# Memory attention and an erf-softplus FFN on one core: batch 0's keys before its values, tokens in chunks of 116 and 112, all heads' sums in one group

## The chip, the cores and the metric

The kernel runs on one core of one Trainium2 chip. TensorE (PE) multiplies, VectorE (DVE), ScalarE (ACT) and GpSimd (POOL) work elementwise, and SyncE (SP) issues the loads and stores, which 16 DMA engines carry out. The metric is the time of one execution on the device in microseconds, lower is better.

## The reference

Eight batches of eight heads, 576 tokens and head size 64 go through an attention over 32 memory slots, and the result through a feed-forward layer with 2048 hidden values.

```python
a = exp(phi - max(phi, axis=2)); a = a / (sum(a, axis=2) + 1e-09)     # phi: b h s 32, max and sum over tokens
k_m = einsum('bhsm,bhsd->bhmd', a, k)
v_m = einsum('bhsm,bhsd->bhmd', a, v)
scores = scale * (q @ k_m.T)                                           # b h s 32
attn = softmax(scores, axis=-1)
x = (attn @ v_m), heads side by side                                   # 4608 x 512
h = x @ w_in                                                           # 4608 x 2048
g = h * erf(softplus(h))
out = g @ w_out                                                        # 4608 x 512
```

Everything is 32-bit floats, and so are the matmuls in effect: most of them are made of three products of high and low parts (`_hi`, `_lo`), some of full 32-bit operands ("exact").

## The kernel before, in words

The kernel is written as a list of operations, each with an engine, a cost in ns, a rank, and the tiles that it reads and writes. A planner (`Plan.order`) plays them through with these costs, always takes the ready operation of lowest rank on the engine that is free first, keeps count of the buffers of each kind (`room`), and so fixes the order of the instructions on every engine before the kernel is built. On the chip each engine runs its list strictly in that order and waits where an operand isn't there. While the first output matmul has not been placed, TensorE's expected gaps are filled with matmuls on zeros (`fill`, L365).

`FIRST` (L821) is the order of the first loads: phi transposed (two halves of the heads), phi, the keys and values of head pairs 0 and 1 (`kv0`, `kv1`), the first eighth of w_in, `kv2`, `kv3`, the queries of the batch's two token halves, then the second eighth of w_in and the first of w_out. All loads and stores are issued by SyncE. A `kv` tile holds keys and values of two heads, `[128, 5, 2, 2, 64]`; `load_tokens` (L393) puts tokens 0 to 511 four to a partition (one piece of 4 KB each) and the last 64 tokens into a fifth chunk of 64 partitions.

`memories` (L485) computes a batch's k_m and v_m: the maxima of phi (L491), exponentials (L514, L516, L521), and then `one_memory` (L530) once for each group of four heads: the sums over tokens on TensorE (L540, five chunks by four heads, keys and values side by side in 128 columns, each head to its own 32 rows of the result), a scaled eviction by ScalarE (L550) and a copy (L552), two transposes (L557), and four evictions into `km` and `vm` (L570, L573). The 32-bit product of one matmul is two instructions, so that a group's sums are 40. For batches 1 to 7 this is done while the FFN of earlier batches runs, and the rank puts it well ahead of its use.

`attention` (L616) makes the scores of one token half (L583 of `q` and `km`) and its softmax, nearly all on VectorE (L629 to L650). `vw` (L594) multiplies `w_in` by `v_m` (L583 of `w_in` and `vm`), so that the FFN's first product is `attn @ (v_m @ w_in)`, `ffn1` (L681). The weights come as 64-bit floats and are turned into 32-bit ones (`decode`: L429, L443, L465 on VectorE, L435, L439 on ScalarE). Softplus and erf are ScalarE's (L704, L709); `g_split` multiplies and splits; `ffn2` (L754) sums the output of 512 tokens of each batch over 16 steps, and `ffn2_rest` the remaining 64 tokens of two batches together from `rest`. For the first 16 steps (`FR2`) these 64 columns are gathered by POOL in `rest_f` (L723) and split by `rest_split` (L745 on ScalarE, L748 on VectorE). `store` evicts and issues the output: into one of two `ot` tiles by ScalarE, and in the last batch in two halves, by ScalarE (L800) and VectorE (L803).

Buffers that matter here: `raw` (four) holds phi, `kv`, later queries, and one part of w_out (`wf`) until `split_wo` has split it; `wo` (eight) holds the weights, and at the start also `kv3` and the first queries; `phiT` has two, `ot` two, and `ps`, the result banks of all small products, four.

Of the kernel before, what the change touches and what calls it, by code (L numbers as in the profile page):

```python
# [237 lines left out]
def tile_memory_attention_then_erf_softplus_ffn(  # L238
# [10 lines left out]
    nc = tc.nc  # L249
# [16 lines left out]
    SC = [(c * P, min(P, S - c * P)) for c in range((S + P - 1) // P)]  # L266
    RAW = 4
# [10 lines left out]
        for n, b, kw in (  # L278
# [9 lines left out]
            ("ot", 2, {}),  # L288
# [6 lines left out]
    room.update({"g_hi": 3, "g_lo": 3, "raw": RAW, "ot": 2, "ps": 4, "sc": 2, "dk": 1, "phiT": 2})  # L295
    room.update({f"pso{d}": 1 for d in range(NT)})
    for n in ("pmx", "psm", "prs"):
# [10 lines left out]
        "ot": ("ot", [P, DM], F32),  # L308
# [18 lines left out]
    def mm(n, exact):  # L327
        return 2 * (2 * n / 2.4 + 2.5) if exact else n / 2.4 + 11.7
# [10 lines left out]
    zeros = const.tile([P, 512], BF16, name="zeros")  # L339
# [21 lines left out]
    def fill(n):  # L361
        if n and not idle:
            idle.append(pools["po"].tile([P, DM], F32, name="idle", tag="pso0"))
        for _ in range(n):
            nc.tensor.matmul(out=idle[0], lhsT=zeros[:, :P], rhs=zeros, start=True, stop=True)  # L365


    def load(rank, key, nbytes, emit):
        op(SP, 60, rank, [], [key], emit, nbytes=nbytes)

    def load_weight(rank, name, c):
# [14 lines left out]
        load(rank, key, P * 8192, emit)  # L386

    def load_phiT(rank, b, g):
        key = tile_("phiT", "phiT", b, g)
        load(rank, key, P * S * 4,  # L390
             lambda: nc.sync.dma_start(out=get(key), in_=phiT[b, g * P : (g + 1) * P, :]))

    def load_tokens(rank, key, src, n_bytes, view):  # L393
        n = S // P
        load(rank, (key, "whole"), S // P * P * n_bytes, lambda: nc.sync.dma_start(
            out=view()[:, :n], in_=src[: n * P].rearrange("(p c) e -> p c e", c=n)))
        load(rank + 0.001, (key, "last"), SC[-1][1] * n_bytes, lambda: nc.sync.dma_start(
            out=view()[: SC[-1][1], n], in_=src[n * P :]))

    def load_phi(rank, b):  # L400
        key = tile_("raw", "phi", b, shape=[P, len(SC), H * M], pool="raw")
        load_tokens(rank, key, phi[b], H * M * 4, lambda: get(key))

    def load_kv(rank, b, p, tag="raw"):
        key = tile_(tag, "kv", b, p, shape=[P, len(SC), 2, 2, D], pool=tag)
        load_tokens(rank, key, kv[b, p], 4 * D * 4,
                    lambda: get(key).rearrange("p c x h d -> p c (x h d)"))

    def load_q(rank, u, tag="raw"):
        key = tile_(tag, "q", u, shape=[P, NP_, U], pool=tag)  # L410
        b, hf = divmod(u, 2)
        load(rank, key, P * NP_ * U * 4, lambda: nc.sync.dma_start(
# [72 lines left out]
    def memories(rank, rank_2, b):  # L485
        a = ("phi", b)
        n, ln = S // P, SC[-1][1]
# [11 lines left out]
        def turn():  # L499
            for g in range(NG):  # L500
# [5 lines left out]
        op(DVE, on_dve(n * H * M), rank, [(a, "whole"), ps], [(a, "whole")],  # L506
           lambda: nc.vector.tensor_tensor(
               out=get(a)[:, :n], in0=get(a)[:, :n],
               in1=get(ps).unsqueeze(1).to_broadcast([P, n, H * M]), op=ALU.add))
        op(DVE, on_dve(H * M), rank, [(a, "last"), ps], [(a, "last")],  # L510
           lambda: nc.vector.tensor_tensor(
               out=get(a)[:ln, n], in0=get(a)[:ln, n], in1=get(ps)[:ln], op=ALU.add))
        op(ACT, on_act(n * H * M), rank, [(a, "whole")], [(a, "whole")],
           lambda: nc.scalar.activation(get(a)[:, :n], get(a)[:, :n], AF.Exp), kind="exp")  # L514
        op(ACT, on_act(H * M), rank, [(a, "last")], [(a, "last")],
           lambda: nc.scalar.activation(get(a)[:ln, n], get(a)[:ln, n], AF.Exp), kind="exp")  # L516
# [10 lines left out]
        for g in range(NG):  # L527
            one_memory(rank_2 + g * 0.01, b, g)

    def one_memory(rank, b, g):  # L530
        a, rs = ("phi", b), ("prs", b, g)
# [180 lines left out]
    def g_split(rank, i):  # L712
# [3 lines left out]
        if i < FR2:  # L716
            t = tile_(("g_hi", "g_lo")[i % 2], "g", i, shape=[P, S], pool="g")
            r = ("rest_f", k // 8)
            if k % 8 == 0:
                tile_("ot", *r)  # L720
# [88 lines left out]
    def at(step):  # L809
        return 100 * step  # L810
# [136 lines left out]
```

## Time and profile before

| | us |
|---|---|
| median of 3 runs | 731.06 (730.51 to 731.53) |
| profiled execution, its own time | 729.75 |
| its span, first to last instruction | 728.0 |

The span is cut by the profile into what each engine did and into the chain of work that ended last, followed back from the last instruction. The granted clock of TensorE is 0.999 of full speed in this execution. Times in the rows are microseconds from the span's start, means of groups are in ns; L540 is line 540 of the kernel. A matmul's row has the shape of the array that it uses (128\*128, 128\*32, 64\*32) and the elements that it produces; `x40` counts instructions. The matmuls on zeros at the start count as busy time.

### The profile page before, as it was taken

What the parts mean: (1) busy time and instruction counts of PE and PEld (TensorE: products, weight loads), DVE (VectorE), ACT (ScalarE), POOL (GpSimd) and SP (SyncE); (2) the same over time, 40 slices, a digit from 0 to 9 for tenths busy, and PEclk for the clock granted to TensorE, in tenths of its full rate; (3) what the DMA queues carried; (4) which work ended last, traced back from release to release, by engine and by line L of the source; (5) the groups of instructions that cost most, each with busy time, mean ns of one, the idle gap of its engine ahead of it and who ended that gap; (6) DMA issues with size and microseconds to landing.
All of it is one profiled execution on the core that took longest, in us unless ns stands there. A gap on an engine that the chain in (4) does not pass through costs nothing.

```text
span 728.0 us, 12307 instructions
## 1 busy us (share of the span) xinstructions
PE 720.0 (99%) x4816; PEld 553.8 (76%) x4816; DVE 521.0 (72%) x963; ACT 449.9 (62%) x708; POOL 98.7 (14%) x246
## 2 busy tenths in 40 slices
PE   9999999999999999999999999999999999999997
PEld 4456555578887888888788887888878788888885
DVE  3899999689677685877755587777854587666631
ACT  5799999875747666594644556474754266454611
POOL 0011001120111111111111011111111111111110
PEclk9999999999999999999999999999999999999999
DMA  9996332421503115111310214211210100010002
GB/s 321 391 389 227 100 149 82 161 100 43 173 24 108 42 39 178 35 59 34 107 57 1 91 48 127 70 59 33 66 33 1 59 15 0 1 45 15 1 1 72
DMA packets 30393, 64.75 MB, mean 89 GB/s; under 512 B 2688, under 2 KB 13440, under 8 KB 29312
## 3 DMA queue, kind: packets, MB, share of 16 engines
q1 hardware_dynamic: 30336, 63.97, 26.1%
q8 instruction: 38, 0.62, 0.4%
q14 instruction: 19, 0.16, 0.1%
HBM read 54.53 MB, written 9.44 MB: 88 GB/s over the span
## 4 chain that ended last, share of the span: by engine, by line
PE 87%; DMA 6%; ACT 4%; DVE 1%; SPq 1%; issue 1%
PE pso L754 48%; PE psh L681 26%; PE psr L754 6%; PE psa L583 5%; DMA w<-w_in 4%; PE psa L540 2%; DMA kv<-kv 2%; ACT w L439 1%; ACT w L435 1%; ACT e L709 0%; ACT L709 0%; PE psa L557 0%; ACT e L704 0%; DVE w L443 0%; ACT vw_hi L354 0%
## 5 line engine op out<-in xcount | busy, mean ns | idle before, releaser
L754 PE MATMUL pso<-wo,g_hi 128*128 128x512 f32 x896 | 280.8, 395 | 0.0
L704 ACT ACTIVATE e<-h 128x576 f32<-128x576 f32 x128 | 88.0, 687 | 171.5 <-DVE h L696 170.9
L754 PEld LDWEIGHTS pso<-wo,g_hi 128*128 128x128 f32 x896 | 160.0, 188 | 31.8 <-issue 6.3
L754 PE MATMUL pso<-wo,g_lo 128*128 128x512 f32 x448 | 176.1, 393 | 0.0
L696 DVE COPY h<-psh 128x288 f32<-128x288 f32 x239 | 107.8, 452 | 42.8 <-PE psh L681 41.2
L681 PE MATMUL psh<-at_hi,vw_hi 128*128 128x288 f32 x496 | 113.7, 310 | 0.0
L681 PE MATMUL psh<-at_hi,vw_lo 128*128 128x288 f32 x496 | 106.0, 295 | 0.3 <-DVE vw_lo L356 0.3
L681 PE MATMUL psh<-at_lo,vw_hi 128*128 128x288 f32 x496 | 106.1, 295 | 0.0
L681 PEld LDWEIGHTS psh<-at_hi,vw_hi 128*128 128x128 f32 x496 | 84.5, 188 | 27.8 <-issue 8.2
L735 POOL CAST rest<-g_hi 128x64 fp32r<-128x64 f32 x112 | 51.1, 457 | 391.3 <-DVE g_hi L730 385.5
L728 DVE TENSOR_TENSOR e<-e,h 128x576 f32<-128x576 f32 x112 | 82.7, 751 | 26.5 <-ACT e L709 26.4
L754 PEld LDWEIGHTS pso<-wo,g_lo 128*128 128x128 f32 x448 | 84.1, 188 | 19.2
L730 DVE CAST g_hi<-e 128x576 fp32r<-128x576 f32 x112 | 50.7, 457 | 63.1 <-PE pso L754 51.1
L731 DVE TENSOR_TENSOR g_lo<-e,g_hi 128x576 fp32r<-128x576 f32 x112 | 86.3, 771 | 4.4
L709 ACT ACTIVATE e<-e 128x576 f32<-128x576 f32 x128 | 80.3, 675 | 0.4
L681 PEld LDWEIGHTS psh<-at_hi,vw_lo 128*128 128x128 f32 x496 | 79.8, 188 | 0.7 <-DVE vw_lo L356 0.5
L681 PEld LDWEIGHTS psh<-at_lo,vw_hi 128*128 128x128 f32 x496 | 79.1, 188 | 0.0
L735 POOL CAST rest<-g_lo 128x64 fp32r<-128x64 f32 x112 | 37.8, 338 | 110.8 <-DVE g_lo L731 103.7
L754 PE MATMUL pso<-w,g 128*128 128x512 f32 x112 | 52.5, 599 | 0.0
L754 PE MATMUL psr<-wo,rest 128*128 128x512 f32 x192 | 49.0, 390 | 0.0
L354 ACT ACTIVATE vw_hi<-psa 128x512 fp32r<-128x512 f32 (+1 forms) x68 | 34.9, 556 | 19.6 <-PE psa L583 19.5
L356 DVE TENSOR_TENSOR vw_lo<-psa,vw_hi 128x512 fp32r<-128x512 f32 (+1 forms) x68 | 42.0, 632 | 6.5 <-ACT vw_hi L354 6.3
(82 smaller groups left out, 716.0 us busy)
## 6 DMA issues: line engine op xcount, KB each, us to landing
kv<-kv SPq DMA_DIRECT2D x32, 512.0 KB, 4.2
q<-qT SPq DMA_DIRECT2D x16, 576.0 KB, 5.0
w<-w_in SPq DMA_DIRECT2D x8, 1024.0 KB, 11.6
w<-w_out SPq DMA_DIRECT2D x8, 1024.0 KB, 11.2
out<-ot SPq DMA_DIRECT2D x32, 256.0 KB, 2.0
phiT<-phiT SPq DMA_DIRECT2D x16, 288.0 KB, 2.9
phi<-phi SPq DMA_DIRECT2D x8, 512.0 KB, 5.7
kv<-kv SPq DMA_DIRECT2D x32, 64.0 KB, 4.2
```

The lines of the kernel that those rows point to most:

```text
L354: lambda: nc.scalar.activation(get_hi(), get_src(), AF.Identity))
L356: lambda: nc.vector.tensor_tensor(out=get_lo(), in0=get_src(), in1=get_hi().bitcast(F32), op=ALU.subtract))
L583: nc.tensor.matmul(out=get(ps[par])[p * M : (p + 1) * M, :], lhsT=w()[rows, p, :], rhs=x()[rows, p, :], start=True, stop=True,)
L681: nc.tensor.matmul(out=get(ps), lhsT=x[:, g, k % 4 * P : (k % 4 + 1) * P], rhs=y[:, g, :], start=(n + g == 0), stop=(n == len(parts) - 1 a ...
L696: lambda: nc.vector.tensor_copy(out=keep(), in_=get(ps)),
L704: last[:] = [op(ACT, on_act(S), rank, [("h", i)], [e], lambda: nc.scalar.activation(get(e), get(("h", i)), AF.Softplus), kind="softplus", ...
L709: last[:] = [op(ACT, on_act(S), rank, [e], [e], lambda: nc.scalar.activation(get(e), get(e), AF.Erf), kind="erf", edge=edge, after=last)]
L728: op(DVE, on_dve(S), rank, [e, h], [e], lambda: nc.vector.tensor_tensor(out=get(e), in0=get(e), in1=get(h), op=ALU.mult))
L730: op(DVE, on_dve(S, 1), rank, [e], [hi], lambda: nc.vector.tensor_copy(out=get(hi), in_=get(e)))
L731: op(DVE, on_dve(S), rank, [e, hi], [lo], lambda: nc.vector.tensor_tensor(out=get(lo), in0=get(e), in1=get(hi).bitcast(F32), op=ALU.subtract))
L735: lambda x=x, y=y: nc.gpsimd.tensor_copy(out=rest[:, k, x, cols], in_=get(y)[:, NT * P :]))
L754: nc.tensor.matmul(out=o, lhsT=y, rhs=z, start=(start and n == 0), stop=(stop and n == len(parts) - 1))
```

## The change

Tokens are laid out in five chunks of 116, 116, 116, 116 and 112 rows: 112 partitions get five tokens each, and the last 16 tokens go to four more partitions with four each. In batch 0 keys and values of a head pair are loaded separately (pieces of 512 bytes), in the order keys, queries, values, with the first eighth of w_in ahead of the keys; `one_memory` takes a list of parts (head group, keys or values), and in batch 0 sums all heads' keys first and all heads' values second, in later batches both groups, keys and values, at once. The evictions of a part write each 64 columns twice side by side, which takes the place of the copy L552, and the evictions into `km` and `vm` take both groups. `raw` has five buffers. The `ot` tiles are gone: outputs pass through `phiT` tiles, and the last batch's stores are one ScalarE copy. `rest_split` is gone: POOL writes the high part of the 64 columns and subtracts for the low part. The planner's cost of a 512-column matmul is 15.5 ns above its columns instead of 11.7.

```diff
-    SC = [(c * P, min(P, S - c * P)) for c in range((S + P - 1) // P)]
-    RAW = 4
+    NC = (S + P - 1) // P
+    FULL = S // NC // 16 * 16
+    MORE = FULL + (S - FULL * NC) // (NC - 1)
+    RAW = 5
...
-    room.update({"g_hi": 3, "g_lo": 3, "raw": RAW, "ot": 2, "ps": 4, "sc": 2, "dk": 1, "phiT": 2})
+    room.update({"g_hi": 3, "g_lo": 3, "raw": RAW, "ps": 4, "sc": 2, "dk": 1, "phiT": 2})
...
-        return 2 * (2 * n / 2.4 + 2.5) if exact else n / 2.4 + 11.7
+        return 2 * (2 * n / 2.4 + 2.5) if exact else n / 2.4 + (15.5 if n == DM else 11.7)
...
+    def load_tokens(rank, key, n_bytes, src, dst, what=None):
+        n = FULL * NC
+        load(rank, n * n_bytes, [(key, (what, "whole")), (key, (what, "last"))],
+             lambda: nc.sync.dma_start(out=dst(slice(0, FULL), slice(0, NC)), in_=src(slice(0, n), NC)))
+        load(rank + 0.001, (S - n) * n_bytes, [(key, (what, "more"))],
+             lambda: nc.sync.dma_start(
+                 out=dst(slice(FULL, MORE), slice(0, NC - 1)), in_=src(slice(n, S), NC - 1)))
...
-        for g in range(NG):
-            one_memory(rank_2 + g * 0.01, b, g)
+        for turn_n, part in enumerate(parts):
+            one_memory(rank_2 + turn_n * 0.01, b, part)
...
+            for n, g in enumerate(gs):
+                for c in range(NC):
+                    ln = MORE if c < NC - 1 else FULL
+                    for j in range(4):
+                        h = 4 * g + j
+                        nc.tensor.matmul(
+                            out=get(ps)[M * j : M * (j + 1), n, : n_x * D],
+                            lhsT=get(a)[:ln, c, h * M : (h + 1) * M],
+                            rhs=get(("kv", b, h // 2))[:ln, c, x0, h % 2 * D : (h % 2 + 1) * D],
+                            start=(c == 0), stop=(c == NC - 1))
...
+            part = [(("rest", k, x), b % 2) for x in range(2)]
+            op(POOL, 400, rank, [t], part[:1], lambda: nc.gpsimd.tensor_copy(
+                out=rest[:, k, 0, cols], in_=get(t)[:, NT * P :]))
+            op(POOL, 400, rank, [t, part[0]], part[1:], lambda: nc.gpsimd.tensor_tensor(
+                out=rest[:, k, 1, cols], in0=get(t)[:, NT * P :],
+                in1=rest[:, k, 0, cols].bitcast(F32), op=ALU.subtract))
...
-    def rest_split(rank, q):
...
-        t = tile_("h" if final else "ot", "ot", *o)
-        halves = [(0, DM // 2, ACT), (DM // 2, DM, DVE)] if final else [(0, DM, ACT)]
+        t = tile_("h" if final else "phiT", "ot", *o)
+        op(ACT, on_act(DM, True), rank - 30, [o], [t],
+           lambda: nc.scalar.activation(get(t)[:, :DM], get(o), AF.Identity))
...
-    FIRST = ["phiT0", "phiT1", "phi", "kv0", "kv1", "in0", "kv2", "kv3", "q0", "q1", "in1", "out0"]
+    BOTH = [(0, 0), (0, 1)], [(1, 0), (1, 1)]
+    TOGETHER = [tuple(BOTH[0] + BOTH[1])]
+    EARLY = [((0, 0), (1, 0)), ((0, 1), (1, 1))]
+    FIRST = ["phiT0", "phiT1", "phi", "in0", "k0", "k1", "k2", "k3", "q0", "q1", "v0", "v1", "v2", "v3"]
+    FIRST += ["in1", "out0"]
...
-    memories(at(-10), at(-9), 0)
+    memories(at(-10), at(-9), 0, EARLY)
...
-        when(n, memories, at(n), at(n + 3), b)
+        when(n, memories, at(n), at(n + 3), b, TOGETHER)
```

176 lines of the change are left out of this document (81 added, 95 removed).

## The prediction

> **What bounds the kernel now.** I read the page first: the span, the busy line and the chain that ended last.
>
> ```profile
> span 728.0 us, 12307 instructions
> ...
> PE 720.0 (99%) x4816; PEld 553.8 (76%) x4816; DVE 521.0 (72%) x963; ACT 449.9 (62%) x708; POOL 98.7 (14%) x246
> ...
> PE 87%; DMA 6%; ACT 4%; DVE 1%; SPq 1%; issue 1%
> ```
>
> TensorE bounds it: 99% busy, and 87% of the chain that ended last is its own work. But the busy share also counts the matmuls on zeros that fill the start (L365), so the start has to be read by itself, from the timeline of TensorE and of VectorE up to 60 us.
>
> ```profile
> 20.19 0.84 PE L583 MATMUL psa<-q,km 64*32 64x288 f32 x16 [0.29 <-DMA q<-qT]
> 22.09 7.73 PE L365 MATMUL idle<-zeros 128*128 128x512 bf16 x35
> 29.66 4.04 PE L681 MATMUL psh<-at,vw_hi 128*128 128x288 f32 x16
> 48.76 1.88 PE L754 MATMUL pso<-w,g 128*128 128x512 f32 x4
> ...
> 21.87 1.37 DVE L632 TENSOR_REDUCE smx<-sc 128x18 f32<-128x576 f32 x2
> 28.26 1.43 DVE L650 STREAM_TRANSPOSE at<-sc 128x576 f32<-128x576 f32 x2
> 31.31 1.22 DVE L465 SCALAR_TENSOR_TENSOR w_in<-w 128x1024 int32<-128x1024 int32 x1
> ```
>
> The columns are start, length, engine, line, operation, tiles, count, and in brackets the idle time and what ended it. The second half of the queries ends the wait at 20.19; then VectorE works through the softmax until 29.69, and only then does the first FFN matmul run. The output matmuls begin at 48.76. So there are two stages: a start of 48.8 us set by loads and by VectorE, and some 679 us in which TensorE is the limit and every microsecond taken off it is a microsecond of time. In that second stage I read the chain in order of time (start, length, what), around the sums of batch 3.
>
> ```profile
> 180.05 1.02 PE psa L583 x16
> 181.07 1.36 PE psa L540 x40
> 182.43 0.90 PE pso L754 x3
> 183.33 0.80 PE psh L681 x6
> 184.13 0.69 PE pso L754 x3
> ...
> 189.27 0.22 PE psa L557 x2
> 189.49 0.69 PE pso L754 x3
> 190.18 1.36 PE psa L540 x40
> 191.54 1.59 PE pso L754 x6
> 193.13 0.22 PE psa L557 x2
> ```
>
> All of it is TensorE, without a gap: two bursts of sums (L540, 40 instructions each) and two pairs of transposes (L557). Three output matmuls take 0.69 us elsewhere and 0.90 us right after a burst (six: 1.59 against 1.38), so leaving a burst costs 0.21 us more. The weight loads show what is inside one burst.
>
> ```profile
> 181.00 0.81 PEld L540 LDWEIGHTS psa<-kv,phi 128*32 128x32 f32 x32 [0.84 <-ACT e L709]
> 182.01 0.15 PEld L540 LDWEIGHTS psa<-kv,phi 64*32 64x32 f32 x8 [0.20 <-issue]
> 182.36 0.30 PEld L754 LDWEIGHTS pso<-wo,g_hi 128*128 128x128 f32 x2 [0.20 <-issue]
> ```
>
> The 32 of the four full chunks go at 0.81 / 32 = 25.3 ns each. Then 0.20 us pass before the 8 of the 64-row chunk (array shape 64*32 instead of 128*32), which go at 18.8 ns, and another 0.20 us before the array is back at 128*128. The 64-row chunk costs 0.35 us of a burst's 1.36, for a tenth of the tokens.
>
> The timeline of TensorE has one pair of transposes like this.
>
> ```profile
> 189.10 0.38 PE L557 MATMUL psa<-ident,kvk 128*128 128x128 f32 x2
> 189.24 0.70 PE L754 MATMUL pso<-wo,g_hi 128*128 128x512 f32 x2
> ```
>
> **The change part by part.** *Sums of batches 1 to 7 in one burst, no 64-row chunk.* Before, per batch: 2 x (1.36 + 0.21) for sums and 2 x 0.22 for transposes = 3.58 us. After: 80 instructions of 116 or 112 rows, all in the shape 128*32. I price them like the 32 full ones, 80 x 25.3 ns = 2.02 us, plus one 0.20 us on leaving, plus 0.21 us of slower output matmuls once. The four transposes stand together: a pair costs 0.22, of which about 0.08 is paid on entering and leaving (the timeline rows above: a pair gives way after 0.14 us, the rest of the 0.22 falls on the matmul after it), so four cost 0.36. Sum 2.79; saved 0.79 per batch, 5.5 us over seven. The bound from below is that only one leave and one pair's entry go and the 80 instructions still take 2 x 1.36: 0.29 per batch, 2.0 us. From above: 0.1 us more per batch for one entry fewer, 6.2 us. I take 5.5, because the 25.3 ns stands in the same burst.
>
> [...]
>
> *What the one burst waits for.* It needs `phi` and all four `kv` tiles at once, all five `raw` slots where it was three tiles for the first burst. A late tile stops TensorE in its order, as one did:
>
> ```profile
> 129.16 1.42 PE L540 MATMUL psa<-kv,phi 128*32 128x128 f32 x36 [0.58 <-DMA kv<-kv]
> ...
> 141.83 0.69 PE L583 MATMUL psa<-q,km 64*32 64x288 f32 x16
> ...
> 149.14 0.62 PE L754 MATMUL pso<-wo,g_hi 128*128 128x512 f32 x2
> ```
>
> Nothing for it in the sum: the sums of batch 3 run at 181 to 192, and TensorE has FFN work that can stand ahead. If that cover is gone it is 0.58 us and more each. In batch 2 the tile `wf` holds a slot too; its sums can only come later than now (121 to 130), after `split_wo` of the last part has freed it. They precede that batch's first queries (141.83 now, which then move as well), and its FFN follows 16 steps behind batch 1's, whose output matmuls begin at 149.14; a step is 2 x 0.80 + 4 x 0.69 = 4.4 us, so there is room. That the wait at 129.16 disappears would give up to 0.6; I count 0.
>
> *The start.* Ahead of the softmax stood phiT 0.59, phi 0.59, keys and values 2.36, the first w_in 1.05 and the queries 1.18 MB. The values' 1.18 MB now come behind the queries. What that is worth, and what the smaller pieces cost, I take from the packets of three windows of the DMA view (15.6 to 17.2, 15 to 16 and 23.4 to 25 us):
>
> ```profile
> DMA packets 498, 0.57 MB, mean 357 GB/s; under 512 B 15, under 2 KB 497, under 8 KB 497
> ...
> DMA packets 286, 0.33 MB, mean 333 GB/s; under 512 B 2, under 2 KB 284, under 8 KB 286
> ...
> q1 hardware_dynamic: 286, 0.33, 106.5%
> ...
> DMA packets 292, 0.63 MB, mean 393 GB/s; under 512 B 3, under 2 KB 3, under 8 KB 286
> ...
> q1 hardware_dynamic: 292, 0.63, 104.3%
> ```
>
> 1.18 MB at 357 GB/s are 3.3 us. The pieces become 512 B (one of keys or values of two heads per token), 2304 of them for the keys, 144 on each of 16 engines. A packet took 1.065 x 16 x 1000 / 286 = 59.6 ns at 1.15 KB and 1.043 x 16 x 1600 / 292 = 91.4 ns at 2.16 KB; the line through both gives 39 ns at 512 B, so 5.6 us for the keys, 2.3 more than at 357 GB/s. The other end is no loss at all. The share above 100% says that the packets overlap and their times are overstated, so I take the middle, 1.1 us for keys and 1.1 for values. The softmax then starts 3.3 - 1.1 = 2.2 us earlier, and all loads behind the values come 2.2 us later. [...]
>
> SyncE issues 16 loads for batch 0's keys and values instead of 8; the second of w_in is queued behind them, and the transfers ahead of it cover the issuing. That w_in is decoded by VectorE at 31.31, after the softmax, so 2.2 us of delay on its landing are hidden. Values at 20.3 + 2.2 us still leave 5 us for their sums, turns and the first `vw`, needed at 29.66 - 2.2. Then VectorE is busy without a break, which lets the gain of 2.2 pass on to 48.76; but ScalarE waits for the fourth w_in:
>
> ```profile
> 28.01 10.14 DMA w<-w_in
> ...
> 38.17 1.11 ACT w L435
> ```
>
> That load comes 2.2 us later, and 1.5 us earlier because batch 1's first `kv` (0.59 MB) no longer finds a free `raw` slot ahead of it: +0.7. Between -2.2 and +0.7 I take -1.2 us for the start, nearer to VectorE's end, since it is VectorE that has no gap there.
>
> *The end.* The last store was VectorE's half, then ScalarE's:
>
> ```profile
> 723.37 0.43 DVE ot L803
> ...
> 723.83 0.38 ACT ot L800
> ...
> L800 ACT ACTIVATE ot<-psr 128x512 f32<-128x512 f32 x3 | 1.7, 581 | 0.0
> ```
>
> 0.84 us becomes one ScalarE copy of 0.58: -0.25.
>
> *Hidden.* `rest_split` goes (two of 0.62 us on ScalarE, two of 0.68 on VectorE), and 16 POOL subtractions come, each behind its copy; bounded by that copy's 0.6 us and its double, on an engine 14% busy, for a result that is read a batch later. ScalarE's 12 evictions of a batch become 6 wider ones on an engine 62% busy. Stores take their tile from the `phiT` slots: a phiT load now waits behind four stores, on SyncE's queue, with `kv` and queries behind it; it is needed a batch later, so 0, and if that cover goes it is the 0.58 us kind of wait above. A planner price of 15.5 instead of 11.7 ns moves orders only.
>
> Sum: -5.5 - 1.2 - 0.25 = -6.95 us. On the profiled execution's 729.75 us (span 728.0) that is 722.8; the median of three runs stands 1.31 higher, so **724.1 us**.
>
> **The rivals.** *Steady gain only.* The fourth w_in sets the start: +0.7 instead of -1.2, 726.0 us. For it: the chain runs through that load. Against: VectorE has no gap from 21.87 on. *The burst does not shrink*, the change not doing what it says: the pace of 80 is set by something other than the shape. 2.0 + 1.2 + 0.25: 727.6 us. Against: the 0.20 us gaps stand on both sides of the 64*32 rows. *The loads go one by one.* By landing times,
>
> ```profile
> kv<-kv SPq DMA_DIRECT2D x32, 512.0 KB, 4.2
> ...
> phiT<-phiT SPq DMA_DIRECT2D x16, 288.0 KB, 2.9
> ```
>
> eight loads of 287 KB at 2.9 us instead of four at 4.2: 6.4 us more until the weights, less 1.5, +4.9 at the start: 731.06 - 5.75 + 4.9 = 730.2 us. Against: 357 GB/s flowed with loads of this size queued behind each other. [...] *Slower: the burst waits for its fourth `kv` tile in every batch.* The tile takes 4.2 us from issue to landing and its slot comes free late, so TensorE stands in its order; from 1.0 us a batch (6.95 / 7) this eats all, and at 1.5 us it gives 724.1 + 10.5 = 734.6 us. For it: 129.16. Against: one such wait in the whole trace. *More:* the start follows by 3.3 and the wait at 129.16 goes: 721.4 us.
>
> **How the numbers follow.** Forecast 0.48, steady only 0.20, burst as before 0.10, more 0.07, one by one 0.06, slower 0.09. Range 720.5 to 729.5 holds all but the last two. Within 0.2% (1.46 us, about what can be told from no change) lies one by one alone: faster 0.85, same 0.06, slower 0.09.
>
> **What would show it.** L540 without any 64*32 form, 80 in one piece of about 2.2 us, and 0.90 us after it only once a batch; the wait for queries ending near 18 us and the first L681 near 27.5; L754 from about 47.5; no L803 at the end. Wrong would be: `kv` as releaser of L540 in several batches, L754 starting after 49, or bursts of 2.7 us.

## The result, and the profile after

The changed kernel is slower: 735.91 us (median of 10 runs, 733.23 to 739.67) against 731.6 us of the kernel before in the same session, a ratio of 1.0065 with a 95% interval of 1.0043 to 1.0086. The forecast was 724.1 us. The profiled execution took 736.58 us by itself. The page of the changed kernel, its span, busy line and shares of the chain that ended last:

```profile
span 734.6 us, 12406 instructions
...
PE 715.7 (97%) x4877; PEld 555.8 (76%) x4877; DVE 518.4 (71%) x955; ACT 435.4 (59%) x654; POOL 101.1 (14%) x262
...
PE 91%; DMA 7%; SPq 0%; ACT 0%; DVE 0%; issue 0%; ACTq 0%
```

TensorE is still the limit of nearly all of it. The timeline of TensorE shows where it is behind (in the new kernel the sums are L563, the transposes L586, the small products L616, the first FFN product L714, the output matmuls L773):

```profile
13.77 0.30 PE L563 MATMUL psa<-kv,phi 116*32 116x64 f32 x4 [0.78 <-ACT w L452]
14.87 0.75 PE L563 MATMUL psa<-kv,phi 116*32 116x64 f32 x36 [0.79 <-DMA kv<-kv]
...
21.16 0.72 PE L616 MATMUL psa<-q,km 64*32 64x288 f32 x16 [0.61 <-DMA q<-qT]
...
32.72 4.12 PE L714 MATMUL psh<-at,vw_hi 128*128 128x288 f32 x16
46.70 0.67 PE L616 MATMUL psa<-w_in,vm 64*32 64x256 f32 x16 [2.24 <-DVE w_in L482]
55.38 1.02 PE L773 MATMUL pso<-w,g 128*128 128x512 f32 x2
61.41 1.30 PE L563 MATMUL psa<-kv,phi 116*32 116x128 f32 x40
64.09 0.41 PE L563 MATMUL psa<-kv,phi 116*32 116x128 f32 x4 [1.38 <-DMA kv<-kv]
66.20 2.35 PE L563 MATMUL psa<-kv,phi 116*32 116x128 f32 x36 [1.70 <-DMA kv<-kv]
165.74 2.40 PE L563 MATMUL psa<-kv,phi 116*32 116x128 f32 x80
```

The queries' wait ends at 21.16 (before: 20.19), although the values no longer stand ahead of the queries. The first output matmul comes at 55.38 instead of 48.76. These 6.6 us are the whole difference of the two spans (734.6 - 728.0; the medians of all runs differ by 4.3). From there on, 679.2 us pass in both kernels, for two reasons that cancel. The one burst of batch 1 stops twice for a late `kv` tile and lasts from 61.41 to 68.48, 7.1 us instead of 2.4. The later bursts save what they should in kind, if not in size. In the chain of waits (start, length, what) stand one burst of batch 3 and its neighbours:

```profile
35.85 16.36 DMA w<-w_in
...
52.23 13.92 DMA kv<-kv
...
193.65 1.38 PE pso L773 x6
195.02 2.33 PE psa L563 x80
197.35 1.79 PE psh L714 x12
199.14 0.44 PE psa L586 x4
```

2.33 for the burst, 0.21 for leaving it (1.79 where twelve such matmuls take 1.58 elsewhere) and 0.44 for the transposes: 2.98 instead of 3.58, so 0.60 us per batch, 4.2 over seven. At its head the chain now runs through 16.4 us of a weight's load and 13.9 us of a `kv` load. That is the clue to the start: the loads are slower. From the DMA view, 4 to 24 us, the kernel before and the changed one:

```profile
DMA packets 3491, 7.46 MB, mean 373 GB/s; under 512 B 238, under 2 KB 1582, under 8 KB 3364
```

```profile
DMA packets 6432, 5.14 MB, mean 257 GB/s; under 512 B 226, under 2 KB 5786, under 8 KB 6431
```

Both are cut to the same 20 us, and 2.3 MB less have come. The late values cost more than their own delay, as ScalarE and VectorE of the changed kernel show:

```profile
27.40 0.62 ACT L578 ACTIVATE kvk<-psa,prs 128x128 f32<-128x128 f32 x2 [7.61 <-PE psa L563]
27.91 1.25 ACT L670 ACTIVATE sc<-sc 128x576 f32<-128x576 f32 x2
...
28.63 1.41 DVE L671 TENSOR_REDUCE ssm<-sc 128x18 f32<-128x576 f32 x2 [3.19 <-ACT sc L670]
```

The softmax's exponentials (L670) stand behind the values' eviction (L578) in ScalarE's fixed list, and that eviction waited 7.61 us for sums over late values. So VectorE idled 3.19 us in the middle of the softmax that the change was meant to bring forward.

### The profile page after: what moved, and what is told of

Same layout as the page of the kernel before. It is cut to its first block, busy times and chain, and to the rows that moved or that the text cites. A ratio compares the mean times of both kernels' runs of the same rounds, so it can differ in the third digit from the quotient of the medians.

```text
span 734.6 us, 12406 instructions
## 1 busy us (share of the span) xinstructions
PE 715.7 (97%) x4877; PEld 555.8 (76%) x4877; DVE 518.4 (71%) x955; ACT 435.4 (59%) x654; POOL 101.1 (14%) x262
## 4 chain that ended last, share of the span: by engine, by line
PE 91%; DMA 7%; SPq 0%; ACT 0%; DVE 0%; issue 0%; ACTq 0%
PE pso L773 49%; PE psh L714 27%; PE psr L773 6%; PE psa L616 5%; DMA kv<-kv 4%; PE psa L563 2%; DMA w<-w_in 2%; DMA q<-qT 1%; PE psa L586 0%; PE idle L366 0%; PE psa L518 0%; SPq L395 0%; DVE ssm L671 0%; SPq L381 0%; ACT kvk L578 0%
## 5 line engine op out<-in xcount | busy, mean ns | idle before, releaser
L773 PE MATMUL pso<-wo,g_hi 128*128 128x512 f32 x896 | 280.5, 394 | 0.0
L773 PEld LDWEIGHTS pso<-wo,g_hi 128*128 128x128 f32 x896 | 160.7, 188 | 33.6 <-issue 6.8
L773 PE MATMUL pso<-wo,g_lo 128*128 128x512 f32 x448 | 176.0, 393 | 0.0
L714 PE MATMUL psh<-at_hi,vw_hi 128*128 128x288 f32 x496 | 114.1, 311 | 0.0
L714 PEld LDWEIGHTS psh<-at_hi,vw_hi 128*128 128x128 f32 x496 | 84.6, 188 | 30.8 <-issue 8.6
L714 PE MATMUL psh<-at_lo,vw_hi 128*128 128x288 f32 x496 | 106.2, 296 | 0.0
L714 PE MATMUL psh<-at_hi,vw_lo 128*128 128x288 f32 x496 | 105.8, 295 | 0.0
L769 POOL CAST rest<-g_hi 128x64 fp32r<-128x64 f32 x112 | 46.7, 419 | 411.8 <-DVE g_hi L764 411.1
L773 PEld LDWEIGHTS pso<-wo,g_lo 128*128 128x128 f32 x448 | 84.1, 188 | 19.2
L714 PEld LDWEIGHTS psh<-at_hi,vw_lo 128*128 128x128 f32 x496 | 79.9, 188 | 0.0
L714 PEld LDWEIGHTS psh<-at_lo,vw_hi 128*128 128x128 f32 x496 | 79.1, 188 | 0.0
L773 PE MATMUL pso<-w,g 128*128 128x512 f32 x112 | 52.6, 602 | 0.0
L773 PE MATMUL psr<-wo,rest 128*128 128x512 f32 x192 | 49.0, 390 | 0.0
L769 POOL CAST rest<-g_lo 128x64 fp32r<-128x64 f32 x112 | 35.4, 316 | 88.1 <-DVE g_lo L765 86.6
```

The costliest lines, as they stand in the source:

```text
L714: nc.tensor.matmul(out=get(ps), lhsT=x[:, g, k % 4 * P : (k % 4 + 1) * P], rhs=y[:, g, :], start=(n + g == 0), stop=(n == len(parts) - 1 a ...
L769: lambda x=x, y=y: nc.gpsimd.tensor_copy(out=rest[:, k, x, cols], in_=get(y)[:, NT * P :]))
L773: nc.tensor.matmul(out=o, lhsT=y, rhs=z, start=(start and n == 0), stop=(stop and n == len(parts) - 1))
```

## The experiments

Three causes were open. A: loads into 112 partitions are slower whatever their pieces. B: the 512-byte pieces, and sixteen loads in place of eight, are slower. C: the order of the work, with steps on the late values ahead of the softmax. Each kernel is timed against the kernel before in its own session (medians 731.45 to 732.1), and the ratio is to that. The diffs are shortened, and the comments in them explain.

**1. Chunks of 128 and 64 rows put back (x1).** All else as changed.

```diff
-        load(rank, n * n_bytes, ..., in_=src(slice(0, n), NC)))        # 112 partitions, five tokens each
+        load(rank, n * n_bytes, ..., in_=src(slice(0, n), NC - 1)))    # 128 partitions, four each; then 64 with one
```

> The changed kernel with one part undone: tokens again as 128 partitions of four and 64 of one; keys and values of batch 0 still separate, all heads' sums still in one group. Theory A (the 112 partitions slow every load that uses them): packets of 4096 B back at 160 ns, those of 512 B at 27 to 30 ns instead of 39, the wait of the sums of batch 1 for kv (3 to 4 us around 61 to 68) gone, the first L773 at 48 or earlier instead of 55.4; about 726 us. Theory B (the 512 B pieces are slow by themselves): 512 B packets stay near 39 ns and the first L773 at 52 or later; only the wait of batch 1 goes, about 731. Theory C (the order of the work, ScalarE's evictions of the values ahead of its exponentials): 512 B packets may be fast, but the first L773 stays at 53 or later; about 733.

731.68 us, ratio 1.000 (0.9986 to 1.0014). The layout alone costs 4 us; what remains is no gain. The burst of batch 1 no longer waits, but the first output matmul comes at 53.22 us, where A alone asked for 48 or earlier: B or C is at work too.

**2. The start put back (x2):** loads, sums and their order of batch 0 as before, chunks of 116 and 112 rows kept.

```diff
-    FIRST = [..., "in0", "k0", "k1", "k2", "k3", "q0", "q1", "v0", "v1", "v2", "v3", "in1", "out0"]
+    FIRST = [..., "kv0", "kv1", "in0", "kv2", "kv3", "q0", "q1", "in1", "out0"]
-    memories(at(-10), at(-9), 0, EARLY)
+    memories(at(-10), at(-9), 0, [tuple(x) for x in BOTH])
```

> The changed kernel with batch 0's loads and sums as before (kv0, kv1, in0, kv2, kv3, queries; two groups), 112 and 116 rows kept. Theory A: 5120 B packets stay at 290 ns or more wherever kv and phi are loaded, queries land near 24 instead of 20.3, first L773 at 52 or later, about 733 to 736. Theory B: no 512 B piece is left, first L773 near 49, about 728. Theory C: as B.

738.75 us, ratio 1.0104 (1.0085 to 1.0123): slower still, and more than A expected, although whole keys and values are loaded again in large pieces. With the slow layout, the changed start as a whole is even the better one, by some 2.8 us.

**3. The kernel before, with 112 partitions of four tokens and one chunk of 128 (x3).** Nothing else of the change is in it.

```diff
-    SC = [(c * P, min(P, S - c * P)) for c in range((S + P - 1) // P)]
+    SC = [(0, 112)] * 4 + [(0, 128)]
```

> The kernel before with one thing changed: the tokens of phi and kv as 112 partitions of four (pieces of 4096 B, as before) and 128 partitions of one, so no 64-row chunk and no 5 KB piece. Theory A: 4096 B packets go from 160 ns to 250 or more, phi and kv of batch 0 take some 4 us longer, first L754 at 52 or later, 733 to 737. A theory that the 5120 B pieces are at fault, not the 112 partitions: 4096 B packets stay at 160 ns, first L754 at 48.8, and with the 64*32 shape gone 2 x 0.3 us a batch are saved: 727.

740.38 us, ratio 1.0112 (1.009 to 1.0134), a larger loss than A's 733 to 737. Its DMA view, 4 to 24 us, its first output matmul and its waits of TensorE:

```profile
DMA packets 3090, 5.45 MB, mean 273 GB/s; under 512 B 211, under 2 KB 1875, under 8 KB 3089
```

```profile
59.63 4.53 PE L755 MATMUL pso<-w,g 128*128 128x512 f32 x10
```

```profile
PE psa L541 <- DMA kv<-kv: 4.3, 4, 1.8
```

The pieces are 4 KB as before (the last chunk has 128 of 1 KB instead of 64), the number of loads is the same, and the rate falls from 373 to 273 GB/s. The first output matmul comes 10.9 us later than the 48.76 of the kernel before, and the two spans differ by 11.1: the loss lies in the start. A is shown without any other part of the change.

The traces also record every packet, and their times narrow A down. From 4 to 24 us a 4 KB packet takes 164 ns (median) in the kernel before and 279 here. After 200 us, where the load of a `kv` tile often comes alone (12 times in each), it takes 159 ns in both; where two such loads follow each other (3 and 4 times), 159 in the kernel before and 213 here. So the rate is lost where several loads of 112 partitions are under way, as at the start, and not by one alone.

**4. Both put back (x4):** chunks of 128 and 64 rows and the start as before. Left of the change are one group, five `raw` slots, stores through `phiT`, GpSimd's split and the wide evictions.

> The changed kernel with both undone: 128 and 64 rows, and batch 0 as before. What is left is the one group of sums of later batches (with two 64-row chunks in it), five raw slots, the stores through phiT slots and the rest columns on POOL. Theory A and B: first L773 near 48.8; per batch one leave of a burst and one pair's entry saved, 0.2 to 0.3 us, and 0.25 at the end: 729.5. Theory C's general form (the other edits reorder the start for the worse): first L773 at 51 or later, over 731.

728.01 us, ratio 0.9949 (0.9934 to 0.9964), faster than both. Its start is ordered as before (first FFN matmul at 31.30, 1.6 us later; first output matmul at 49.17, 0.4 later; 7.04 MB in 4 to 24 us). Its burst, in the weight loads of TensorE:

```profile
185.28 0.81 PEld L562 LDWEIGHTS psa<-kv,phi 128*32 128x32 f32 x32 [0.36 <-ACT e L736]
186.29 0.15 PEld L562 LDWEIGHTS psa<-kv,phi 64*32 64x32 f32 x8 [0.20 <-issue]
186.64 0.81 PEld L562 LDWEIGHTS psa<-kv,phi 128*32 128x32 f32 x32 [0.20 <-issue]
187.66 0.15 PEld L562 LDWEIGHTS psa<-kv,phi 64*32 64x32 f32 x8 [0.20 <-issue]
```

In the chain it takes 2.73 us.

**5. The planner told of slower loads (x5).** The kernel of experiment 1, but the planner prices loads of keys or values alone at 1.6 times their bytes; only the order of instructions changes.

```diff
-        op(SP, 60, rank, [], keys, emit, nbytes=nbytes)
+        op(SP, 60, rank, [], keys, emit, nbytes=nbytes * slow)   # slow = 1.6 for keys or values alone
```

> The changed kernel with chunks of 128 and 64 rows (731.68 us), and only the planner is told that a load of keys alone or of values alone costs 1.6 times its bytes. On ScalarE the values' first eviction then stands behind both softmax exponentials instead of between them and ahead of the second, and on VectorE the second w_in's decode stands behind the last softmax transpose. No instruction is added or removed but zero matmuls. Theory C (the gain of early keys is lost to the planned order, in which work on late loads stands ahead of the softmax): no eviction of values between the exponentials, no wait of 3.4 us of TensorE for the queries' softmax, first FFN matmul near 30 us instead of 32.2, first output matmul 2 to 3 us earlier than 53.2, about 729 us. Rival (the loads themselves come too late: second w_in at 28.5 us instead of 23, later weights with it, and FFN steps wait for them in any order): first output matmul stays at 53, 731.7 us.

731.03 us, ratio 0.9986 (0.9974 to 0.9998), not told apart from experiment 1. The first FFN matmul came at 29.35 and the first output matmul at 51.74 (53.22 in experiment 1): the order gave back 1.5 us of the start, about half of what C asked for, and the time hardly moved.

**6. The 64-row chunks of both groups next to each other (x6),** in the kernel of experiment 4.

```diff
-                for c in range(NC):
+                turns = list(range(NC)) if n % 2 == 0 else [NC - 1] + list(range(NC - 1))
+                for c in turns:
```

> The fastest so far (chunks of 128 and 64 rows, the start of the kernel before, the other parts of the change; 728.01 us) with one edit: in a burst the second head group begins with its 64-row chunk, so that the 64-row chunks of both groups stand next to each other and the array changes its shape twice a burst less. Theory of the prediction (each change of shape costs 0.20 us): the burst of 80 falls from 2.80 to about 2.5 us, seven times 0.28, 726.0 us. Rival (the 64-row chunk is slow itself, or the pace is set by something other than the shape): 2.80 stays, 728.0 us.

727.61 us, ratio 0.9946 (0.9933 to 0.9959).

```profile
185.00 0.81 PEld L563 LDWEIGHTS psa<-kv,phi 128*32 128x32 f32 x32 [0.36 <-ACT e L737]
186.01 0.37 PEld L563 LDWEIGHTS psa<-kv,phi 64*32 64x32 f32 x16 [0.20 <-issue]
186.59 0.81 PEld L563 LDWEIGHTS psa<-kv,phi 128*32 128x32 f32 x32 [0.20 <-issue]
```

The burst falls by 0.14 us in the chain (2.59), half of what was expected: sixteen short ones in a row take 0.37, not twice 0.15. So the 18.8 ns of the prediction's row (0.15 / 8) was too low a pace for 64 rows; 0.37 / 16 is 23 ns. Why eight go at less, no row shows. The time itself can't tell 1.0 us from none here.

**7. Two groups in later batches (x7),** in the kernel of experiment 4.

```diff
-        when(n, memories, at(n), at(n + 3), b, TOGETHER)
+        when(n, memories, at(n), at(n + 3), b, [tuple(x) for x in BOTH])
```

> The fastest so far (728.01 us) with one edit: later batches sum their heads in two groups again, as before the change, so that two bursts of 40 and two pairs of transposes stand in a batch. What is left of the change is five raw slots, stores through phiT, the 64 columns split by GpSimd, the wide evictions and the planner's price. By the rows (two bursts of 1.36 and 0.21 each, 0.44 for transposes, against 2.80, 0.21 and 0.44) one group is worth 0.13 us a batch, so 728.9 us. Rival (one group is what makes that kernel 4 us faster than before): 731 to 732 us. Rival (the groups give nothing, waits differ): 728.0.

730.99 us, ratio 0.999 (0.9981 to 0.9998). Without one group, 3 of the 4 us are gone. By the chain I get 1.4 (3.58 against 2.73 + 0.21 + 0.44, seven times), and 0.8 more from one wait of an output matmul for a weight in its profile; the last 0.8 is within what the two intervals leave open. The other parts that stay (slots, stores, GpSimd's split, evictions) are worth 1 us at most.

**8. Chunks of 128, 128, 128, 96 and 96 rows (x8),** else as experiment 4.

```diff
-        n = MORE * (NC - 1)                  # 128 partitions, four tokens; then 64 partitions, one
+        n = MORE * 3                         # 128 partitions, three tokens; then 96 partitions, two
```

> The fastest so far (728.01 us) with one edit: chunks of 128, 128, 128, 96 and 96 rows: two thirds of the tokens go to 128 partitions with three each, one third to 96 partitions with two each. No chunk has 64 rows, and no load goes to 112 partitions. The burst of 80 should take 2.3 us as with 116 and 112 rows, 0.44 less, 3.1 over seven. Theory A (any load into fewer than all 128 partitions goes at a lower rate): a third of the bytes is slowed as all were with 112 partitions (10.7 us of the total), so +3.6 - 3.1: 728.5 us, with first-25-us packets of 2 KB on these loads clearly over 85 ns. Rival (only 112 is bad, since it is not a multiple of 32, and 96 is served at full rate): 724.9 us.

730.45 us, ratio 0.9978 (0.9968 to 0.9989). The burst is one shape, 80 weight loads in 2.13 us as with 116 rows, and yet the kernel is 2.4 us slower than experiment 4. Its DMA view from 4 to 24 us:

```profile
DMA packets 3392, 6.45 MB, mean 322 GB/s; under 512 B 223, under 2 KB 1247, under 8 KB 3352
```

With a third of these bytes in loads of 96 partitions the rate is 322 GB/s, where experiment 4 had 352. That is weak evidence by itself, since the kernel before had 373 with the same loads as experiment 4, and the pieces are smaller here (3 and 2 KB). The packets point the same way: a 3 KB packet takes 121 ns where its load comes alone and 153 from 4 to 24 us, a factor of 1.26; for the 4 KB packets of experiment 4 it is 1.16 (159 and 184 ns). The next experiment says more by its time.

**9. The fifth chunk summed over 128 rows, the unused 64 set to zero by GpSimd (x9),** in batches 1 to 7 of experiment 4.

```diff
+    def blank(rank, key, n):
+        op(POOL, 500, rank, [], [(key, (None, "blank"))], lambda: nc.gpsimd.memset(get(key)[FULL:, NC - 1], 0.0))
...
-                    ln = MORE if c < NC - 1 else FULL
+                    ln = MORE if c < NC - 1 or b else FULL
```

> The kernel with chunks of 128 and 64 rows and the start of the kernel before (728.01 us), with one addition: in batches 1 to 7 GpSimd writes zeros into the 64 unused rows of the fifth chunk of phi and of the four kv tiles (35 fills of 64x256), and the fifth chunk is summed over all 128 rows. No load changes and no chunk has another array shape. If the shape changes of the 64-row chunk cost what the weight loads show (80 in one piece 2.33 us against 2.73), this gives 7 x 0.40 = 2.8 us: 725.2 us, and no step of the prediction on the bursts is wrong but its size. Rival: the fills wait for their slots on GpSimd and hold up the low parts of g behind them, or the sums: 728 or more, with GpSimd as a releaser of the sums or of the output matmuls.

726.77 us, ratio 0.9937 (0.9925 to 0.9949).

```profile
184.06 2.32 PE psa L570 x80
```

No matmul waits for the fills. The seven bursts are 2.9 us shorter than those of experiment 4 (2.32 against 2.73 each). The span (724.3) is 2.2 us shorter; the ratios of the two sessions put the gain at 0.9, with intervals that allow 2.2 as well as none. Experiment 8 has the same burst, and its loads of 96 partitions leave it 3.7 us behind this kernel (3.0 by the ratios). No 64-row chunk, without any odd load: this is how the gain of the bursts can be had.

**10. Keys and values in loads of their own, 512-byte pieces, in the order of before (x10),** else as experiment 4.

```diff
-    FIRST = [..., "kv0", "kv1", "in0", "kv2", "kv3", "q0", "q1", ...]
+    FIRST = [..., "k0", "v0", "k1", "v1", "in0", "k2", "v2", "k3", "v3", "q0", "q1", ...]
```

> The same kernel of 728.01 us with one edit: in batch 0 each tile's keys and values are two loads in pieces of 512 bytes, the values right behind the keys, and both groups are summed as before; only the pieces and the number of loads change, not the order of the work. Theory B (the pieces and the sixteen loads cost): keys and values at about 285 GB/s instead of about 340, 2.36 MB in 8.3 us instead of 6.9, so the softmax starts 1.4 us later, 729.4 us, and up to 731.7 if all that early keys lost is this. Theory C (the order of the work behind the late values costs, not the pieces): 728.0 us, packets of 512 bytes at 30 ns or less.

731.71 us, ratio 1.0004 (0.9994 to 1.0014): as much as experiment 1 had lost against experiment 4, though the instructions of ScalarE and VectorE stand in the order of experiment 4 for the first 46 us.

```profile
DMA packets 6933, 5.67 MB, mean 284 GB/s; under 512 B 336, under 2 KB 6032, under 8 KB 6933
```

Two slices of 4 us show two things:

```profile
8.00:12.00 4.00, 2.79 (x40) 1.00 0.98 269
16.00:20.00 4.00, 1.90 (x22) 1.00 0.86 231
```

The columns are the slice, its length, TensorE's busy time and matmuls, its granted clock, the DMA engines' busy share and GB/s. So both the pieces (269 GB/s with the engines busy for 0.98 of the slice) and gaps between loads (0.86) may be at work.

**11. The same with pieces of 2 KB (x11).** Keys and values lie apart in the input array and in the tile; the unused rows are zero as in experiment 9, which is its measure. The whole `kv` loads of later batches have two pieces of 2 KB per partition instead of one of 4 KB by this.

```diff
-            tile_(tag, *key, shape=[P, NC, 2, 2 * D], pool=tag)
+            tile_(tag, *key, shape=[P, 2, NC, 2 * D], pool=tag)
-        .reshape(B, H // 2, S, 4 * D)
+        .reshape(B, H // 2, 2, S, 2 * D)
```

> The fastest so far (chunks of 128 and 64 rows with the unused rows zero, the start of the kernel before; 726.77 us), in which keys and values lie apart in the input array and in the kv tile, so that a load of keys alone comes in pieces of 2 KB; in batch 0 keys and values are two loads each, values right behind the keys, both groups summed as before. It is the kernel that took 731.71 us (3.7 over its parent) but for the size of the pieces (and the zero rows). If the pieces of 512 bytes were what cost: 726.8 us, 340 GB/s or more in the first 20 us. If the number of loads (sixteen in place of eight, eight in flight at most) was: 730.5 us, with the DMA share well under 1 in some slice of the first 20 us, as it was 0.86 from 16 to 20 us.

729.74 us, ratio 0.9984 (0.9971 to 0.9997).

```profile
DMA packets 4045, 6.11 MB, mean 306 GB/s; under 512 B 344, under 2 KB 1944, under 8 KB 4033
```

```profile
8.00:12.00 4.00, 3.11 (x44) 1.00 0.83 221
```

Of the 3.7 us, 3.0 remain with pieces four times as large, and the DMA engines have a hole (a share of 0.83). SyncE's own rows (SPq) show where it comes from: first one pair of issues (start, length), then its longest waits of the first 20 us (total, times, longest).

```profile
2.75 0.58 SPq L400 DMA_DIRECT2D kv<-kv  x1
3.37 0.48 SPq L402 DMA_DIRECT2D kv<-kv  x1
```

```profile
SPq L402 <- DMA w<-w_in: 1.4, 1, 1.4
SPq L400 <- DMA phi<-phi: 1.3, 1, 1.3
```

A pair of loads, 288 KB here, takes SyncE 1.14 us (the next pair starts at 3.89). At that pace 259 GB/s are issued (an estimate from these rows), less than the 351 GB/s that flow in experiment 9, whose pairs carry twice as much. And twice SyncE waits until an earlier load has landed. So most of B goes with the number of loads, not with pieces of 512 bytes. Pieces of 2 KB in whole loads were not run, so a part of the 3.0 us may still be theirs.

**12. Early keys with pieces of 2 KB (x12):** the order of the change in the kernel of experiment 11.

```diff
-    FIRST = [..., "k0", "v0", "k1", "v1", "in0", "k2", "v2", "k3", "v3", "q0", "q1", "in1", "out0"]
+    FIRST = [..., "in0", "k0", "k1", "k2", "k3", "q0", "q1", "v0", "v1", "v2", "v3", "in1", "out0"]
-    memories(at(-10), at(-9), 0, [tuple(x) for x in BOTH])
+    memories(at(-10), at(-9), 0, EARLY)
```

> The same tile and array with keys and values apart and pieces of 2 KB, and now the order of the change: in01 first eighth of w_in, keys, queries, values, keys summed first and values second in batch 0. This is what the prediction thought the start would be (softmax 2 to 3 us earlier, weights about as before). Prediction's step on the start, with the pieces made good: 1 to 2 us under 726.8, about 725.3 us. Rival (sixteen loads cost by themselves): 729 to 730. Rival (the order costs: the values come late, TensorE and ScalarE wait for the first vw, as the wait of 1.4 us for vw_hi showed when the planner was told of slower loads): 727 to 729, with vw_hi or the values' tile as releaser in front of the first FFN matmul.

729.01 us, ratio 0.9963 (0.9949 to 0.9976). Here the softmax did come early: its maxima start at 19.30 us, 2.6 before the 21.87 of the kernel before. Then, on ScalarE and TensorE:

```profile
27.26 1.19 ACT L454 ACTIVATE w<-w 128x1024 int32<-128x1024 uint32 x1 [3.54 <-DMA w<-w_in]
28.34 0.54 ACT L602 ACTIVATE vm<-psa 64x128 f32<-64x128 f32 x2
...
28.64 1.40 PE L618 MATMUL psa<-w_in,vm 64*32 64x256 f32 x16 [3.79 <-DVE sc L678]
31.23 5.49 PE L716 MATMUL psh<-at,vw_hi 128*128 128x288 f32 x16
```

ScalarE's list has the decode of the second w_in (L454) ahead of the eviction of `vm`. The w_in is late, so `vm` is, and TensorE stands for 3.79 us. (The releaser that the row names, on VectorE, is the last by the profile; the one that the product needs is `vm`.)

**13 and 14. The same kernel with the planner told of later landings (x13, x14):** keys and values at 1.6 times their bytes, the second w_in at 1.4 times (x13) or 1.8 times (x14).

```diff
-        load(rank, P * 8192, [key], emit)
+        load(rank, P * 8192, [key], emit, slow=1.4 if (name, c) == ("in", 1) else 1.0)    # 1.8 in x14
```

> The kernel with early keys in pieces of 2 KB (729.01 us), and only the planner is told that keys and values cost 1.6 times their bytes and the second w_in 1.4 times. On ScalarE the values' eviction and the first vw eviction then stand ahead of the second w_in's decode, and on VectorE the whole softmax does. If the order was the loss: no wait of 3.8 us in front of the first vw, first FFN matmul at 28 us or before instead of 31.2, first output matmul near 49 instead of 53.4, and 1 to 2 us under the best so far (726.77): 725.3 us. If the start is set by the weights' loads in any order: first output matmul at 51 or later, 728 to 729.

> The same with the second w_in told at 1.8 times: the high part of the first token half's softmax stands ahead of its decode too, and the FFN's first evictions ahead of later decodes. Same numbers expected if the order was the loss (725.3 us, or 0.5 less); 728 to 729 if the loads set the start. If this one is slower than the other, the decode of weights is what is late next.

729.66 us, ratio 0.996 (0.9946 to 0.9973), and 726.26 us, ratio 0.9929 (0.9918 to 0.9941). Only the number told to the planner differs between the two, and by it the order of the instructions and whether ScalarE or VectorE does some small ones. 3.4 us lie between the medians, 2.3 by the ratios. The timeline of TensorE in the faster one:

```profile
27.89 4.04 PE L717 MATMUL psh<-at,vw_hi 128*128 128x288 f32 x16
...
46.88 1.88 PE L776 MATMUL pso<-w,g 128*128 128x512 f32 x4
...
57.47 1.10 PE L776 MATMUL pso<-w,g 128*128 128x512 f32 x2 [1.94 <-ACT w L459]
```

The first FFN matmul at 27.89 and the first output matmul at 46.88 are 1.8 and 1.9 us earlier than before. Then the output matmuls wait 1.94 us for a weight that ScalarE decodes late, and give it all back. The slower one has the same first output matmul (46.91) and then waits 2.89 us for that weight, and 2.4 us more for decodes of w_in. Experiment 14 is the fastest kernel measured, but not told apart from experiment 9, which leaves the start alone.

## Why the prediction was wrong, step by step

*The step that failed* is the price of the loads in "The start": "1.18 MB at 357 GB/s are 3.3 us", and with it the line through two packet sizes, which prices the pieces by their size alone. No term asks what a load into 112 partitions costs, although the layout moves every load of phi, keys and values to 112 partitions, in all batches; this was put at nothing without a reason. Experiment 3 shows that this one thing costs 8 us in the kernel before. Between experiments 2 and 4, at the same start, it costs 10.7 us (738.75 against 728.01); in the changed kernel 4.2 (against experiment 1). The forecast missed by 11.8 us.

What it is in a load of 112 partitions that costs the time, no run here shows. Measured are 273 GB/s with 112 partitions (experiment 3) against 373 with 128 (the kernel before) and nearly the same pieces, and 213 ns for a 4 KB packet against 159 where two loads follow each other.

*The pieces and the number of loads.* The prediction took 1.1 us for the keys' pieces between 0, an end that no run shows, and 2.3. Experiments 10 and 11 give 3.7 us for small pieces and more loads together, in keys and values, of which 3.0 stay when the pieces are 2 KB. That "the transfers ahead of it cover the issuing" is what failed here: SyncE's 1.14 us for a pair of loads is longer than the 0.83 us that the pair's 0.29 MB take at 357 GB/s. The 39 ns that the line gave for a packet of 512 bytes is the median in the changed kernel, but by luck: that is its slow layout, and with 128 partitions such a packet takes 32 ns (experiment 1) or 27 (experiment 10). The mechanism of the rival "the loads go one by one" was the right one in part; its 4.9 us, at a chance of 0.06, are near the measured 3.7.

*The softmax 2.2 us earlier* was right, where the loads allow it: 2.6 us in experiment 12, and in experiment 14 the first FFN matmul at 27.89 (foretold near 27.5) and the first output matmul at 46.88 (about 47.5). That the gain would stay was wrong. VectorE, of which the prediction says that it "has no gap there", has two short ones in the kernel before, 0.24 us at 32.77 and 0.38 at 38.17, the second for the same late w_in that ScalarE waits for. That "all loads behind the values come 2.2 us later" was priced at one load, the fourth w_in; the second w_in, which I called hidden behind the softmax, blocked ScalarE for 3.54 us in experiment 12, and a later weight took 1.94 in experiment 14. The step left out what stands behind a waiting instruction in ScalarE's list: the values' eviction behind a decode in experiment 12, and in the changed kernel the softmax's own exponentials behind the values' eviction.

*The bursts.* Right in kind, one shape and one exit. The 80 take 2.33 us in the chain, with the change of shape behind them, instead of 2.02 + 0.20, and the four transposes 0.44 instead of 0.36, as two pairs did: no gain from standing together. Saved are 0.60 us per batch and 4.2 in all, instead of 0.79 and 5.5. The 25.3 ns came from 32 instructions with a change of shape behind them; 80 in one piece go at 2.13 / 80 = 26.6 ns:

```profile
165.74 2.13 PEld L563 LDWEIGHTS psa<-kv,phi 116*32 116x32 f32 x80 [0.36 <-DVE e L762]
```

*The wait for the fourth kv tile* came, in batch 1 alone: 1.38 and 1.70 us in the rows above. That burst lasts 4.7 us longer than a later one, the sums that run slower behind the waits included. In batches 2 to 7 no burst waits. "There is room" held for them; batch 1, whose loads share the engines with the weights at the start, was not looked at by itself.

*The end* was right: from the end of the last matmul to the end of the span 4.67 us before (728.0 - 723.33) and 4.37 after (734.6 - 730.23), 0.30 saved against 0.25.

*Hidden.* In the changed kernel no wait of TensorE names GpSimd's columns or the stores. ScalarE does wait for stores' tiles, 11.8 us in all, off the path.

The parts together: experiment 9 has the steady gain and the end without the new loads, and is 4.7 us under the kernel before (731.5 - 726.77), where the chain gives 4.2 and 0.3. Experiment 4 is 4.1 under it (732.1 - 728.01), of which the chain shows 1.4 for its bursts, 0.3 for the end and 0.6 for the wait of before at 129.16; the other 1.8 I did not locate. Layout and separate loads then cost 7.9 us on top (735.91 - 728.01, two sessions; 8.5 by the ratios).

## What to carry to other kernels

A layout that suits one engine (no 64-row chunk for TensorE) was paid for here by the transfers that fill it (273 GB/s with 112 partitions in experiment 3, 373 with 128), above all where many were under way at once: look at the partitions of each load before the count of its matmuls, and pad on the chip instead (experiment 9, a ratio of 0.9937). Splitting a load in two also doubles the issues, and a pair of those took SyncE 1.14 us (experiment 11). Where the order of instructions is fixed ahead, a late load can cost what is queued behind its first reader on that reader's engine, and not only its own delay: in experiment 12 ScalarE stood 3.54 us for the second w_in, and TensorE 3.79 us for the `vm` queued behind that decode; one landing time told to the planner moved the same kernel by 2 to 3 us (experiments 13 and 14). Price a change of the start on every load up to steady state, not on the one that the chain names.

## What the hardware showed that was not expected

The rate of loads by partitions: 373 GB/s with 128, 273 with 112 at nearly the same pieces (from 4 to 24 us, kernels before and x3), 322 with a third of the keys, values and phi in loads of 96 (x8). One load of 112 partitions alone shows no loss: 159 ns for a 4 KB packet as with 128.

Two stretches of waiting cost more than their length, because the granted clock was lower behind them. TensorE in the kernel of experiment 12, in slices of 4 us (busy time, matmuls, granted clock, DMA share, GB/s):

```profile
24.00:28.00 4.00, 0.85 (x4) 0.91 0.99 374
28.00:32.00 4.00, 3.36 (x21) 0.50 1.02 413
```

After 3.79 idle us the clock was 0.50, and 16 matmuls took 5.49 us that take 4.04 in experiment 14, where the clock was 1.00 from 28 to 32 us. In the changed kernel it was lower behind two waits in batch 1 too, of 1.38 us (to 64.09) and 1.70 us (to 66.20), and 1.00 again from 72 to 76 us:

```profile
64.00:68.00 4.00, 2.21 (x38) 0.76 1.04 368
68.00:72.00 4.00, 4.00 (x26) 0.81 1.04 386
```

How long a wait has to be for that, no run here shows; behind one of 1.00 us at 16.32 in the changed kernel it stayed at 1.00 (16 to 24 us). In the kernel before matmuls on zeros stand where the softmax of the start leaves TensorE without work (35 of them, 7.73 us from 22.09 on), and the clock is 1.00 in every slice from 4 to 32 us. They are placed ahead of the first output matmul alone and where the planner expects a gap, and none stands in the waits above.
